# One overlapping read for the normalised tiles, and q, k, v weights in two row blocks of 256

## The chip, the cores and the metric

The kernel runs on one core of a Trainium2 chip. The metric is the time of one execution in microseconds of device time (us); lower is better. A core has engines with instruction queues of their own: PE (TensorE, matrix multiplication), DVE (VectorE), ACT (ScalarE), POOL (GpSimd) and SP (SyncE, which here only issues DMA transfers). They run at the same time and wait for each other through semaphores. A DMA transfer is issued by a queue (SP's or ACT's) and is then carried out by 16 DMA engines; who needs its data waits until the last share has landed.

## The reference

Two blocks share one normalised input, and both results are added to the input. S is 2048 tokens, D is 448 columns, 16 heads of 28 columns, a window of 256 tokens, F is 1792.

```python
def _A_ref(x, wqkv, wo):
    B, S, D = x.shape
    H = 16; Dh = D // H; W = 256
    qkv = (x @ wqkv).reshape(B, S, 3, H, Dh).transpose(2, 0, 3, 1, 4)
    q, k, v = qkv[0], qkv[1], qkv[2]
    scores = jnp.einsum("bhqd,bhkd->bhqk", q, k) * (Dh ** -0.5)
    idx = jnp.arange(S)
    mask = (idx[:, None] - idx[None, :] >= 0) & (idx[:, None] - idx[None, :] < W)
    p = softmax(jnp.where(mask[None, None], scores, -1e9))
    o = jnp.einsum("bhqk,bhkd->bhqd", p, v)
    return o.transpose(0, 2, 1, 3).reshape(B, S, D) @ wo

def _B_ref(x, w_gate, w_up, w_down):
    return (gelu(x @ w_gate) * (x @ w_up)) @ w_down

xn = _layernorm(x)
return x + _A_ref(xn, A_wqkv, A_wo) + _B_ref(xn, B_w_gate, B_w_up, B_w_down)
```

All tensors are bfloat16; sums are kept in float32.

## The kernel before, in words

**Tiling.** The tokens are 16 tiles of 128 rows (`x_sb`), handled in four blocks of 512 tokens (`qb` 0 to 3). A tile is normalised (`norm`, L169) into `xn`, turned by 90 degrees into `xnT` (128 partitions x 4 chunks x 2048 tokens), and `xnT` then feeds every matmul that contracts over the 448 columns of x. 448 is seven pieces of 64, while a partition dimension holds two pieces. So three chunks of `xnT` hold pieces 0 to 5 in pairs, and chunk 3 holds piece 6 in both halves. Of a contraction over 448, three matmuls take 128 rows each and one takes the last 64. Two such last halves, of different outputs, stand in the two halves of the array at once: one uses the upper copy of piece 6, the other the lower copy. For the feed-forward matmuls and for the projections of blocks 1 to 3, all seven pieces run as 64-row matmuls, two outputs beside each other; there each half of the array needs all seven pieces, its own ones from `xnT` and the other half's from `xsw`, a copy of `xnT` with the halves exchanged, which DMA makes (`swap`, L479). `wvs` and `wsq` are the weights for these exchanged pieces.

**How piece 6 comes into both halves.** For tiles 4 to 15, `norm` writes 512 columns with two DVE instructions (L174): 448 columns, and then the last 64 once more. The tile is turned by a DMA transpose (`dma_transp`, L186). For tiles 0 to 3 only 448 columns are written; PE turns them (`transp`, L190), the fourth transpose reading columns 320 to 447, and then POOL copies piece 6 from the upper to the lower half for all four tiles (L779, 64 x 512).

**Weights.** `wv` holds the v weights, `wraw` the q and k weights as loaded, both with four chunks. `wqp`, `wkp` and `w3p` hold q and k again, with each head padded from 28 to 32 columns: `pads` (L747) copies three chunks for groups of four heads, L790 copies the last 64 rows into `w3p`. The four spare columns of each padded head carry the last heads; `fill_pads` (L292) writes these, out of `wraw` and out of the small tile `w3k`.

**The first loads.** SP issues, in this order: tile 0 of x, tiles 2 and 3 (ACT issues tile 1), `wv` rows 0 to 383, the q and k columns of the first four heads (rows 0 to 383), tiles 4 to 7 of x in one transfer (L92), then the rows 384 to 447 of q, k and v (L94, L96; four transfers of 64 rows, v's twice), the other columns of q and k (L98), `wu`, and the two halves of `w3k`. Eight semaphores tell of landings in turn, so that a transfer is issued only when the one eight places ahead has landed (DMAHW0 to DMAHW7 in the lists below).

**Order of work.** Everything runs on one written order (a manual schedule). It begins with ten matmuls on zeros (`warmup`), statistics and normalisation of tiles 0 to 3 on DVE, their transposes on PE, v for tiles 0 to 3 (`v_dense` for three chunks, `v_half` for the fourth), q and k of the first four heads (`proj`, `qk_halves`), and then attention of block 0. In between DVE computes the statistics of tiles 4 and 5 (`stat`, L153, written before `qk_halves`). From there PE alternates between scores (L686), the product with v (L660) and pieces of other matmuls that a plan deals out. Tiles 4 to 7 are normalised during attention of block 0, tiles 8 to 11 in its feed-forward part, tiles 12 to 15 in that of block 1.

## Time and profile before

| | |
|---|---|
| median of 3 runs | 211.53 us (211.53 to 211.76) |
| the profiled execution | 211.63 us, of which its span is 209.9 us |
| PE busy | 204.2 us (97% of the span) |
| DVE busy | 156.4 us (75%) |
| ACT busy | 134.9 us (64%) |
| POOL busy | 42.0 us (20%) |
| DMA | 15.68 MB in 24890 packets, 9208 of them under 512 B |

The span runs from the first to the last instruction of the profiled execution; 1.73 us of its time lie around it. The granted PE clock stands at 9 tenths or more in all 40 slices. The DMA engines are nearly full from 2 us to about 20 us, and lightly loaded after 60 us. A row of the list in order of time gives the start, the time from the first start to the last end, the engine, the line, the operation, what it writes and reads, the shape and how many instructions are merged; behind it stands, in brackets, how long the engine had been idle and what ended that. PE's matmuls are pipelined, so their durations overlap.

### The profile page before, as it was taken

To read this page: it belongs to the slowest core of one execution; us is meant where nothing else is said; L and a number is where in the kernel's file an instruction comes from. 1 tells how busy PE (TensorE), PEld (TensorE's weight loads), DVE (VectorE), ACT (ScalarE), POOL (GpSimd) and SP (SyncE) were. 2 spreads that over 40 slices of the span, in tenths; PEclk is the share of its full clock that TensorE was granted. 3 is DMA by queue.
4 is the path that set the end of the run, shared out by engine and by line. 5 is a ranking of instruction groups with operands and counts; after the bars stand their busy time and mean duration, and the time that the engine had idled before them with its cause. 6 is when DMAs were issued, how large, how long until landed. Compare 5 with 4: busy or idle time off the path is not lost. (4 is left out here: it accounts for less than half of the span.)

```text
span 209.9 us, 6659 instructions
## 1 busy us (share of the span) xinstructions
PE 204.2 (97%) x2837; PEld 98.0 (47%) x2842; DVE 156.4 (75%) x359; ACT 134.9 (64%) x133; POOL 42.0 (20%) x77
## 2 busy tenths in 40 slices
PE   7899999999999999999999999999999999999994
PEld 2343444544454545444445444544444454544572
DVE  6898899899788984797438897395385699596532
ACT  4799896866677977423777788522587787756000
POOL 5368902241000220040000102012000022041000
PEclk9999999999999999999999999999999999999999
DMA  6999789983341001003331000100000010100011
GB/s 170 277 233 217 148 179 222 283 263 72 84 107 40 25 22 22 8 5 70 71 76 47 25 3 25 22 3 22 22 3 0 5 47 3 48 5 16 3 47 50
DMA packets 24890, 15.68 MB, mean 75 GB/s; under 512 B 9208, under 2 KB 24728, under 8 KB 24856
## 3 DMA queue, kind: packets, MB, share of 16 engines
q1 hardware_dynamic: 24712, 15.10, 31.2%
q8 instruction: 23, 0.38, 0.8%
q10 hardware_dynamic: 144, 0.11, 0.2%
q14 instruction: 11, 0.09, 0.2%
HBM read 9.26 MB, written 2.41 MB: 56 GB/s over the span
## 5 line engine op out<-in xcount | busy, mean ns | idle before, releaser
L691 ACT ACTIVATE p_sb<-sc 128x2048 bf16<-128x2048 f32 x38 | 71.4, 1879 | 16.9 <-PE sc L686 11.7
L543 ACT ACTIVATE p_sb<-gt 128x1024 bf16<-128x1024 f32 x28 | 28.6, 1026 | 31.3 <-PE gt L503 26.9
L503 PE MATMUL gt<-xnT,wg 64*128 64x512 bf16 x224 | 45.6, 376 | 0.0
L626 POOL TENSOR_TENSOR oN<-oc,l 128x512 bf16<-128x512 f32 x16 | 20.7, 1298 | 121.6 <-DVE l L639 121.6
L412 PE MATMUL po<-wd,hT 128*128 128x448 bf16 (+1 forms) x224 | 44.7, 347 | 0.0
L503 PE MATMUL gt<-xsw,wg 64*128 64x512 bf16 x168 | 40.7, 376 | 0.0
L611 DVE TENSOR_TENSOR p_sb<-p_sb,masks 128x256 bf16<-128x256 bf16 (+1 forms) x98 | 30.9, 369 | 7.4 <-ACT p_sb L691 7.4
L553 DVE TENSOR_TENSOR hT<-p_sb,u 128x512 bf16<-128x512 bf16 x34 | 21.7, 675 | 13.3 <-PE u L503 13.3
L412 PEld LDWEIGHTS <-hT 128*128 128x128 bf16 x238 | 21.9, 98 | 19.1 <-issue 2.2
L503 PEld LDWEIGHTS <-wg 64*128 64x128 bf16 x392 | 19.0, 94 | 22.3
L503 PEld LDWEIGHTS <-wu 64*128 64x128 bf16 x392 | 18.7, 94 | 22.2 <-issue 0.4
L503 PE MATMUL u<-xnT,wu 64*128 64x512 bf16 x136 | 28.1, 376 | 0.0
L503 PE MATMUL u<-xsw,wu 64*128 64x512 bf16 x102 | 24.7, 376 | 0.0
L503 PE MATMUL ue<-xnT,wu 64*128 64x512 bf16 x88 | 18.0, 377 | 0.0
L645 DVE TENSOR_TENSOR oc<-oc,ov 128x512 f32<-128x512 f32 (+1 forms) x16 | 10.4, 656 | 10.0 <-ACT oc L643 9.9
L503 PE MATMUL ue<-xsw,wu 64*128 64x512 bf16 x66 | 16.3, 377 | 0.0
L686 PE MATMUL sc<-qT,kT 28*64 28x320 bf16 (+4 forms) x736 | 16.2, 259 | 0.0
L400 DVE TENSOR_TENSOR res<-po,x_sb 128x448 bf16<-128x448 f32 (+1 forms) x14 | 8.1, 605 | 7.8 <-PE po L412 6.7
L686 PEld LDWEIGHTS <-kT 28*64 28x64 bf16 x736 | 8.1, 103 | 12.2 <-issue 11.0
L520 DVE CAST hT<-ue 128x512 bf16<-128x512 f32 x16 | 10.5, 685 | 2.8 <-PE ue L503 2.8
L643 ACT COPY oc<-ov 128x512 f32<-128x512 f32 x16 | 9.3, 585 | 4.0 <-PE ov L660 4.0
L639 DVE STREAM_TRANSPOSE l<-inv_all 128x512 f32<-128x512 f32 x16 | 11.1, 702 | 0.1
(115 smaller groups left out, 253.2 us busy)
## 6 DMA issues: line engine op xcount, KB each, us to landing
out_dram<-res SPq DMA_DIRECT2D x15, 112.0 KB
wd<-in_B_w_down_dram SPq DMA_DIRECT2D x2, 784.0 KB
x_sb<-in_A_x_dram SPq DMA_DIRECT2D x3, 448.0 KB
xsw<-xnT SPq DMA_DIRECT2D x6, 192.0 KB
wg<-in_B_w_gate_dram SPq DMA_DIRECT2D x2, 560.0 KB
wu<-in_B_w_up_dram SPq DMA_DIRECT2D x4, 224.0 KB
wu<-in_B_w_up_dram SPq DMA_DIRECT2D x2, 336.0 KB
wraw<-in_A_wqkv_dram SPq DMA_DIRECT2D x2, 252.0 KB
```

The lines of the kernel that those rows point to most:

```text
L412: nc.tensor.matmul(po[:, 0:w], lhsT=x[:, k, tt * P:(tt + 1) * P], rhs=wt[:, k, lo:up], start=start and n == 0, stop=stop and n == len(term ...
L503: nc.tensor.matmul(ps, lhsT=w[64 * hi:64 * hi + 64, c, p * P:(p + 1) * P], rhs=xchunk(qb, hi, c, qb * QB, QB), start=c == 0, stop=c == 6, ...
L520: copy(out=hTs[qb][:, p + 7 * i, :], in_=us[i])
L543: nc.scalar.activation(out=ges[p][:, :, :], in_=gt[:, :, :], func=ACT.Gelu_apprx_tanh)
L553: nc.vector.tensor_tensor(out=hT[:, p + 7 * i, :], in0=ge[:, i, :], in1=u, op=ALU.mult)
L611: nc.vector.tensor_tensor(out=reg, in0=reg, in1=m, op=ALU.mult)
L626: nc.gpsimd.tensor_tensor(out=oN[:, g, :], in0=oc[:, :], in1=inv, op=ALU.mult)
L639: nc.vector.transpose(out=l1[:, :, :], in_=inv_all[:, 4 * qb + g, :].unsqueeze(2).to_broadcast([P, 16, 32]))
L643: nc.scalar.copy(out=oc[:, :], in_=ov[0][:, :])
L645: nc.vector.tensor_tensor(out=oc[:, q0:], in0=oc[:, q0:], in1=ov[1][:, q0:], op=ALU.add)
L686: nc.tensor.matmul(ss[k0:k0 + nk, j, col:col + nq], lhsT=kT[r, g, kt * P + k0:kt * P + k0 + nk], rhs=qT[r, g, ring(qb).start + q0:ring(qb) ...
L691: nc.scalar.activation(out=p_sb[:, :, 0:ncol], in_=ss[:, :, 0:ncol], func=ACT.Exp, scale=SCALE)
```

## The change

The seven pieces of 64 columns are laid out anew. A tile of 512 columns now holds columns 192 to 447 and then columns 0 to 255, so that piece 3 (columns 192 to 255) stands twice: in the lower half of chunk 0 and in the upper half of chunk 3. (Before, piece 6 stood in both halves of chunk 3.)

For tiles 4 to 15 `norm` is one DVE instruction whose input pattern reads the tile in two rows of 256 columns, the second starting 192 columns before the first. For tiles 0 to 3 it still writes 448 columns, and the four PE transposes start at columns 192, 320, 0 and 128; POOL's copy at L779 is gone. Contractions that use the one half take chunks 0 to 2 whole and the low half of chunk 3; the others take chunks 1 to 3 whole and the high half of chunk 0. So q and even v tiles use the first form, k and odd v tiles the second.

The weights follow: one helper, `qkv`, loads rows 192 to 447 into chunks 0 and 1 and rows 0 to 255 into chunks 2 and 3, for v, and for the first and the other columns of q and k. The 64-row transfers and `w3k` are gone. Each of q, k and v thus has 512 rows loaded instead of 448. `w3p` is filled by `pads3`, one instruction for each half: the first four heads by ACT (two copies of 64 x 112), the other twelve by POOL (two of 64 x 336), where one ACT copy of 128 x 448 stood. `wvs` is copied from `wv` on the chip, and no longer loaded from memory. Which pieces are a half's own changes in the tables `OWN` and `SWAPPED`; the number of matmuls of each form stays the same.

```diff
+OWN = ({3: 0, 5: 1, 0: 2, 2: 3}, {4: 0, 6: 1, 1: 2, 3: 3})
+SWAPPED = ({4: 0, 6: 1, 1: 2}, {5: 0, 0: 1, 2: 2})
...
+    def qkv(dst, c0, c1):
+
+        for i in range(2):
+            nc.sync.dma_start(out=dst[:, 2 * i:2 * i + 2, :], in_=A_wqkv[192 - 192 * i:448 - 192 * i, c0:c1].rearrange("(c p) n -> p c n", p=P))
+
+    def columns(lo, up, k):
+
+        qkv(wraw[:, :, k * D + lo:k * D + up], k * D + lo, k * D + up)
+
...
-    nc.sync.dma_start(out=wv[:, 0:3, :], in_=rows(A_wqkv, 0, 3)[:, :, 2 * D:3 * D])
-    for c in (0, D):
-        nc.sync.dma_start(out=wraw[:, 0:3, c:c + 4 * Dh], in_=wqk[:, :, c:c + 4 * Dh])
+    qkv(wv, 2 * D, 3 * D)
+    columns(0, 4 * Dh, 0)
+    columns(0, 4 * Dh, 1)
     nc.sync.dma_start(out=x_sb[:, 4:8, :], in_=xv[:, 4:8, :])
-    for a in range(2):
-        nc.sync.dma_start(out=wraw[64 * a:64 * a + 64, 3, 0:D], in_=A_wqkv[384:448, a * D:(a + 1) * D])
-    for a in range(2):
-        nc.sync.dma_start(out=wv[64 * a:64 * a + 64, 3, :], in_=A_wqkv[384:448, 2 * D:3 * D])
-    for c in (0, D):
-        nc.sync.dma_start(out=wraw[:, 0:3, c + 4 * Dh:c + D], in_=wqk[:, :, c + 4 * Dh:c + D])
+    for k in range(2):
+        columns(4 * Dh, D, k)
...
-    w3k = const.tile([P, 4 * Dh], bf16, name="w3k")
-    for a in range(2):
-        nc.sync.dma_start(out=w3k[64 * a:64 * a + 64, :], in_=A_wqkv[384:448, D + 12 * Dh:2 * D])
...
-        xf = xn[:, :, :].rearrange("p a b -> p (a b)")
-        both = ((0, D, 0), (D, 64, 384))
-        for lo, n, src in both if t > 3 else both[:1]:
-            nc.vector.tensor_scalar(out=xf[:, lo:lo + n], in0=x_sb[:, t, src:src + n], scalar1=mv_all[:, t, 0:1],
-                                    scalar2=rstd_all[:, t:t + 1], op0=ALU.subtract, op1=ALU.mult)
+        x = x_sb[:, t, :]
+        to = xn[:, :, :].rearrange("p (i a) b -> p i (a b)", i=2)
+        if t > 3:
+            x = bass.AP(x.tensor, x.offset + 192, [list(x.ap[0]), [-192, 2], [1, 256]])
+        else:
+            x, to = x, xn[:, :, :].rearrange("p a b -> p (a b)")[:, 0:D]
+        nc.vector.tensor_scalar(out=to, in0=x, scalar1=mv_all[:, t, 0:1], scalar2=rstd_all[:, t:t + 1], op0=ALU.subtract, op1=ALU.mult)
...
-        for c, lo in enumerate((0, P, 2 * P, D - P)):
+        for c, lo in enumerate((192, 320, 0, P)):
...
     def v_dense(t, pv, first=True):
-        mm3(pv, lambda c: xnT[:, c, t * P:(t + 1) * P], lambda c: wv[:, c, :], first, not first)
+        m = t % 2
+        mm3(pv, lambda c: xnT[:, m + c, t * P:(t + 1) * P], lambda c: wv[:, m + c, :], first, not first)
...
+    def pads3(gs, eng=nc.gpsimd.tensor_copy):
+
+        for hi in range(2):
+            r, hs, c0 = slice(64 * hi, 64 * hi + 64), slice(4 * gs.start, 4 * gs.stop), D * hi
+            src = wraw[r, 3 - 3 * hi, c0 + Dh * hs.start:c0 + Dh * hs.stop]
+            eng(out=w3p[r, hs, 0:Dh], in_=src.rearrange("p (h d) -> p h d", d=Dh))
...
-    nc.gpsimd.tensor_copy(out=xnT[0:64, 3, 0:QB], in_=xnT[64:128, 3, 0:QB])
...
-    nc.scalar.copy(out=w3p[:, :, 0:Dh], in_=wraw[:, 3, 0:D].rearrange("p (h d) -> p h d", d=Dh))
+    pads3(slice(0, 1), nc.scalar.copy)
     nc.vector.memset(masks[:, 0, 0, 0:1], 1.0)
     make_masks(slice(0, 6))
+    pads3(slice(1, 4))
...
-        wv64 = A_wqkv[0:3 * P, 2 * D:3 * D].rearrange("(c h p) n -> h p c n", h=2, p=64)
         for hi in range(2):
-            nc.sync.dma_start(out=wvs[64 * hi:64 * hi + 64, :, :], in_=wv64[1 - hi])
+            nc.sync.dma_start(out=wvs[64 * hi:64 * hi + 64, :, :], in_=wv[64 - 64 * hi:P - 64 * hi, hi:hi + 3, :])
```

SP's queue at the start of the program, before the change. The words in brackets are what an instruction waits for; a transfer that waits for DMAHW0 to DMAHW7 waits for the landing of the one eight places ahead.

```order
1 L85 DMA x_sb<-in_A_x_dram 128x448
2 L88 DMA x_sb<-in_A_x_dram 128x2x448
3 L89 DMA wv<-in_A_wqkv_dram 128x3x448
4 L91 DMA wraw<-in_A_wqkv_dram 128x3x112 x2
5 L92 DMA x_sb<-in_A_x_dram 128x4x448
6 L94 DMA wraw<-in_A_wqkv_dram 64x448
7 L94 DMA wraw<-in_A_wqkv_dram 64x448 [waits DMAHW0_49]
8 L96 DMA wv<-in_A_wqkv_dram 64x448 [waits DMAHW1_49]
9 L96 DMA wv<-in_A_wqkv_dram 64x448 [waits DMAHW2_49]
10 L98 DMA wraw<-in_A_wqkv_dram 128x3x336 [waits DMAHW3_49]
11 L98 DMA wraw<-in_A_wqkv_dram 128x3x336 [waits DMAHW4_49]
```

The same place after the change:

```order
1 L95 DMA x_sb<-in_A_x_dram 128x448
2 L98 DMA x_sb<-in_A_x_dram 128x2x448
3 L89 DMA wv<-in_A_wqkv_dram 128x2x448 x2
4 L89 DMA wraw<-in_A_wqkv_dram 128x2x112 x3
5 L89 DMA wraw<-in_A_wqkv_dram 128x2x112 [waits DMAHW0_49]
6 L102 DMA x_sb<-in_A_x_dram 128x4x448 [waits DMAHW1_49]
7 L89 DMA wraw<-in_A_wqkv_dram 128x2x336 [waits DMAHW2_49]
8 L89 DMA wraw<-in_A_wqkv_dram 128x2x336 [waits DMAHW3_49]
9 L89 DMA wraw<-in_A_wqkv_dram 128x2x336 [waits DMAHW4_49]
10 L89 DMA wraw<-in_A_wqkv_dram 128x2x336 [waits DMAHW5_49]
```

Tiles 4 to 7 of x move from the sixth place on SP's queue to the ninth, behind 112 KiB more of v weights and 56 KiB more of q and k weights.

POOL's queue around the masks of block 0, before the change (`lnv` and `rstd_all` are the inverse deviation of tile 5):

```order
12 L779 COPY xnT<-xnT 64x512 [waits DVE_49,Activation_49,Pool_49]
13 L115 AFFINE_SELECT masks<-masks 64x64 [waits DVE_49]
14 L115 AFFINE_SELECT masks<-masks 64x4x64 x3
15 L115 AFFINE_SELECT masks<-masks 64x64
16 L115 AFFINE_SELECT masks<-masks 64x4x64
17 L161 TENSOR_SCALAR lnv<-mv_all 128x1 [waits DVE_49,Pool_49]
18 L162 TENSOR_TENSOR rstd_all<-lnv,minus_half 128x1 [waits Pool_49]
```

And after it:

```order
12 L121 AFFINE_SELECT masks<-masks 64x64 [waits DVE_49]
13 L121 AFFINE_SELECT masks<-masks 64x4x64 [waits Pool_49]
14 L121 AFFINE_SELECT masks<-masks 64x4x64 x2
15 L121 AFFINE_SELECT masks<-masks 64x64
16 L121 AFFINE_SELECT masks<-masks 64x4x64
17 L766 COPY w3p<-wraw 64x12x28 [waits DMAHW3_49]
18 L766 COPY w3p<-wraw 64x12x28 [waits DMAHW4_49]
19 L164 TENSOR_SCALAR lnv<-mv_all 128x1 [waits DVE_49,Activation_49,Pool_49]
20 L165 TENSOR_TENSOR rstd_all<-lnv,minus_half 128x1 [waits Pool_49]
```

A copy ahead of the masks is gone, and two copies stand between the masks and the deviation of tile 5; each of them waits for a landing of `wraw`.

43 lines of the change are left out of this document (23 added, 20 removed).

## The prediction

> **What bounds the kernel now.** I read the page's slices first: is one engine full all the way, and where not?
>
> ```profile
> PE   7899999999999999999999999999999999999994
> ```
>
> PE is below nine tenths only in the first two slices (10.5 us) and in the last. Since a pipelined PE is shown busy a little too long, I then asked for the waits of PE alone, longest first (us in total, times, longest):
>
> ```profile
> PE wps L150 <- DVE wo L124: 1.4, 1, 1.4
> PE tp L197 <- ACT xn L182: 0.8, 1, 0.8
> PE pk L202 <- issue: 0.2, 1, 0.2
> PE pq L202 <- issue: 0.2, 1, 0.2
> ```
>
> These are all its waits: two at the start (before the warm-up, and for tile 1), and 0.4 us afterwards. So whatever makes DVE, POOL, SP or the DMA engines cheaper later on has at most 0.4 us to win, and the end moves only with what PE waits for at the start. The third view is therefore the list in order of time from 6.4 us, all engines:
>
> ```profile
> 6.41 0.40 PE L197 MATMUL tp<-ident,xn 128*128 128x128 bf16 x4 [0.83 <-ACT xn L182]
> 6.75 0.74 PE L202 MATMUL pv<-wv,xnT 128*128 128x448 bf16 x3
> 7.54 0.27 DVE L752 COPY wqp<-wraw 128x336 bf16<-128x336 bf16 x1
> 8.14 0.42 DVE L198 COPY xnT<-tp 128x512 bf16<-128x512 bf16 x1 [0.33 <-PE tp L197]
> 8.23 0.47 ACT L752 COPY wkp<-wraw 128x336 bf16<-128x336 bf16 x1
> 8.49 0.63 DVE L155 BATCH_NORM_STATS2 st<-x_sb 128x6 f32<-128x448 bf16 x1
> 8.62 0.82 PE L202 MATMUL s<-xnT,wqp 128*128 128x512 bf16 x3
> 8.73 0.61 POOL L779 COPY xnT<-xnT 64x512 bf16<-64x512 bf16 x1 [3.17 <-ACT wkp L752]
> 8.90 0.56 ACT L790 COPY w3p<-wraw 128x448 bf16<-128x448 bf16 x1 [0.19 <-DMA wraw<-in_A_wqkv_dram]
> 9.15 0.18 DVE L156 BATCH_NORM_AGGREGATE mv_all<-st 128x2 f32<-128x6 f32 x1
> 9.25 0.59 DVE L155 BATCH_NORM_STATS2 st<-x_sb 128x6 f32<-128x448 bf16 x1
> 9.37 0.29 ACT L164 ACTIVATE lnv<-mv_all,eps_t 128x1 f32<-128x1 f32 x1
> 9.41 2.18 POOL L115 TENSOR_SCALAR_AFFINE_SELECT masks<-masks 64x64 bf16<-64x64 bf16 x6
> 9.70 0.20 ACT L165 ACTIVATE rstd_all<-lnv 128x1 f32<-128x1 f32 x1
> 9.88 0.18 DVE L156 BATCH_NORM_AGGREGATE mv_all<-st 128x2 f32<-128x6 f32 x1
> 10.02 0.39 PE L208 MATMUL s<-xnT,w3p 64*128 64x512 bf16 x2
> 10.48 0.69 DVE L256 CAST kT<-s 128x512 bf16<-128x512 f32 x1 [0.41 <-PE s L208]
> 11.27 0.44 DVE L752 COPY wkp<-wraw 128x336 bf16<-128x336 bf16 x1
> 11.39 0.42 PE L686 MATMUL sc<-qT,kT 28*64 28x320 bf16 x16
> ```
>
> From 6.41 us PE has work without a break. The reader is to see what nearly holds it up. The first scores at 11.39 need `kT`, which DVE casts from 10.48 to 11.17; ahead of that cast, in DVE's order, stand the statistics of tiles 4 and 5 (8.49 to 10.06), whose input is the transfer that the change puts behind more weights. Now DVE waits 0.41 us for PE before the cast; that is the cover.
>
> **The change, part by part.** *Tiles 4 to 7 of x land later.* Their statistics start at 8.49 without a wait, so I take 8.49 as the landing, its latest. If they start at t, DVE needs 1.39 to the second aggregate (8.49 to 9.88), 0.10 to its next instruction (9.15 to 9.25), 0.69 for the cast, and PE follows DVE by 0.06 (8.56 to 8.62): scores at t + 2.24. The branch over ACT (Ln at t + 0.88, Exp, then the cast of `qT`, under 0.7) comes to about t + 2.1 and is not the longer one. Scores at 11.39 hold while t is at most 9.15: the cover is 0.66 us.
>
> Ahead of this transfer stand 112 KiB more for `wv` and 56 KiB more for q and k, 172 kB. What the DMA engines moved, by stretch (the last two columns are their busy share and GB/s):
>
> ```profile
> 0.00:6.10 6.10, 4.14 (x14) 1.42 (x14) 3.97 (x16) 2.79 (x6) 3.24 (x9) 1.00 0.68 184
> 3.40:3.90 0.50, 0.50 (x2) 0.15 (x1) 0.47 (x3) 0.00 (x0) 0.26 (x1) 1.00 0.91 178
> 3.90:6.10 2.20, 1.68 (x9) 0.53 (x7) 2.13 (x6) 1.50 (x5) 0.27 (x1) 1.00 0.98 270
> 6.25:6.75 0.50, 0.34 (x4) 0.23 (x5) 0.44 (x2) 0.47 (x4) 0.00 (x0) 1.00 1.08 359
> 6.70:8.50 1.80, 1.80 (x16) 0.95 (x14) 1.34 (x5) 1.68 (x6) 0.00 (x0) 1.00 0.95 253
> ```
>
> 172 kB take 0.64 us at 270 GB/s and 0.68 at 253, the two stretches in which `wv`, the first q and k columns and these tiles themselves move. So t is 9.13 to 9.17, and the scores are delayed by 0 to 0.02 us. The ends are 359 GB/s (0.48 us, no delay) and 178 (0.97 us, a delay of 0.31). I take 0.05 us, near the two middle rows, since a late landing costs and an early one gives nothing. Being issued later costs nothing by itself: SP needs about 0.5 us a transfer,
>
> ```profile
> 2.24 1.02 SPq L91 DMA_DIRECT2D wraw<-in_A_wqkv_dram  x2
> 3.30 0.49 SPq L92 DMA_DIRECT2D x_sb<-in_A_x_dram  x1
> ```
>
> so three more put it at about 4.9 to 5.4 us; 1.15 MB are queued ahead of it by then, and the engines had moved 1.12 MB only by 6.1 us (184 GB/s over 6.1 us), so they do not run dry. The wait of the second first-columns transfer of k is for tile 0 of x, which DVE has been reading since 3.05.
>
> A row that bears on the price: the q and k columns come in pieces of 224 bytes.
>
> ```profile
> DMA packets 601, 0.21 MB, mean 275 GB/s; under 512 B 487, under 2 KB 601, under 8 KB 601
> DMA packets 225, 0.18 MB, mean 359 GB/s; under 512 B 28, under 2 KB 225, under 8 KB 225
> ```
>
> The first row is the stretch 4.50 to 5.25, mostly such pieces, the second 6.25 to 6.75, nearly none: a quarter less, not half. The Trainium skill ("DMA: Bandwidth & Descriptors", Specifications) says that a piece under 512 B does not reach line rate, because it is read, modified and written; this speaks against loading more of them. If each piece of 224 bytes cost as much as one of 512, an estimate from that page, the 256 additional pieces would count for 131 kB instead of 57, the landing would come 0.29 us later at 253 GB/s, and the sum below would be 211.8 instead of 211.6. The first row does not bear that out.
>
> *v weights in two blocks.* `v_dense(0)` at 6.75 reads both blocks, its third matmul, some 0.4 us later, the second one. x and `wv` are 0.92 MB after the change, of 1.12 MB moved by 6.1: no wait, though the slowest share may come near. `pads` of q at 7.54 and of k at 8.23 follow 0.2 and 0.4 us of data behind: no wait.
>
> *ACT's `w3p`.* One copy (0.56) becomes two of 112 columns; by 336 and 448 columns (0.47, 0.56) a copy of 112 is about 0.29, two 0.58. The wait of 0.19 for the 64-row transfer goes, so they end at 9.3 (9.46 before); PE wants the result at 10.02.
>
> *POOL.* The copy of 0.61 is gone and the masks start near 8.6 and end near 10.8. The two copies of `w3p` are at most 0.61 each (the row of 512 columns), and wait for the other q and k columns. These had landed by 11.27 (`wkp` there ran without a wait); 112 KiB more, 115 kB at 253 GB/s, is 0.45: by 11.72 at the latest. POOL is done by 12.4 or so, and PE wants it here, at 13.72:
>
> ```profile
> 12.97 0.81 PE L202 MATMUL pk<-xnT,wkp 128*128 128x512 bf16 x3
> 13.72 0.39 PE L208 MATMUL pq<-xnT,w3p 64*128 64x512 bf16 x1
> ```
>
> Behind the copies wait the deviation of tile 5, which the second of the four norms ahead of the transposes reads, and the masks on the first exponentials, which nobody on PE reads before the scores of the next steps are through. *DVE's `wkp`* of the second group, now at 11.27, waits by the same 0.45 and ends at 12.2; PE wants it at 12.97. Queued behind it are a v cast and the copies for groups 3 and 4 (the row of 12.16 below); they run 0.45 later, and PE comes to them only after 13.72.
>
> *The overlapping read.* The group rows (count, then busy and mean ns):
>
> ```profile
> L174 DVE TENSOR_SCALAR xn<-x_sb,mv_all,rstd_all 128x448 bf16<-128x448 bf16 x15 | 6.9, 460 | 0.1
> L174 DVE TENSOR_SCALAR xn<-x_sb,mv_all,rstd_all 128x64 bf16<-128x64 bf16 x12 | 5.1, 429 | 0.0
> 12.16 0.38 DVE L752 COPY wqp<-wraw 128x672 bf16<-128x672 bf16 x1
> ```
>
> Twelve instructions go (5.1 us of DVE). The remaining ones grow by 64 columns: 0.02 us each by the copies of 336 and 672 columns (0.27, 0.38), 0.43 at worst, if the pattern breaks the rate. DVE wins 0 to 0.4 us a tile, 0.3 likely. Four of the tiles come ahead of the DMA transposes of block 1, eight in the gated parts; PE waits for neither. What hides it: the last exchanged copy of block 1 is issued here, and read here,
>
> ```profile
> 25.66 1.25 SPq L484 DMA_DIRECT2D xsw<-xnT  x2
> 30.50 0.48 PEld L337 LDWEIGHTS <-xsw 64*128 64x128 bf16 x6
> ```
>
> 3.6 us after the issue has ended. *`wvs`* from the chip and three transfers fewer on SP lie under the same cover. *PE* has as many matmuls of each form as before.
>
> **Sum.** The profiled execution took 211.63 us, span 209.9, 0.10 above the median of 211.53. Delay 0.05, nothing won on the path: span about 209.95, 211.6 for the median.
>
> **The rivals.** *Slower: x lands too late.* The same transfer, with a landing after 9.57 us (8.49 + 0.66 + 0.42), from which point the delay passes 0.42 us. For it: 178 GB/s where `wv` begins to move, and 16 shares of which the slowest counts. Against it: the other four rows. At 129 GB/s, below any row, it lands at 9.82 and the time is 212.2. *Slower: the overlapping read is slow.* Each of the four norms ahead of the transposes would have to take some 1 us more than the pair it replaces to use up the cover of 3.6 us; beyond it the time is 211.6 plus the rest, about 212.1 at 4.1 us. Against it: no row of this form does so. *Faster: PE's remaining waits go.* Both rows of 0.2 us vanish since DVE and SP are less loaded: 211.1. Against it: "issue" says that they wait for nothing shown, and no part of the change touches them.
>
> **How the numbers follow.** What can be told from no change is about 0.2%, 0.42 us. Forecast, no measurable change, 211.6: 0.73. Late x: 0.17. Slow read: 0.04. Faster: 0.06. That gives faster 0.06, same 0.73, slower 0.21. The range must reach 211.84 (the end of the unknown price) and further into the late landing, to 212.2; downwards half of the faster rival, 211.2. The likeliest case alone is 211.4 to 211.9.
>
> **What would show it.** Right: the statistics of tile 4 start between 9.0 and 9.3 and now wait for `x_sb`; the first scores at 11.4 to 11.5; norms of 512 columns near 0.40 us where nothing disturbs them; POOL's `w3p` copies over before 13; no new PE wait. Wrong: a PE wait for `wv` at 6.75 or 7.1, scores after 11.8, a PE wait for `xsw` near 29, or a span that moves without any of these.

## The result, and the profile after

The changed kernel is slower. In the first comparison its median was 212.26 us (212.07 to 212.87, 8 runs) against 211.56 us for the kernel before, a ratio of 1.0036 (95% interval 1.0026 to 1.0046). In a later comparison it was 212.00 us (211.83 to 212.25, 9 runs) against 211.52, a ratio of 1.0022 (1.0012 to 1.0032). So it loses 0.5 to 0.7 us. (Two executions far off, 300.61 us of the kernel two_norms and 1167.99 us of before_pool3, are left out of the medians and ranges below.) The forecast was no measurable change, at 211.6 us. The profiled execution took 212.47 us, span 210.7, 0.8 above the span before.

PE is as full as it was (the same 40 digits). The waits of PE alone, longest first (us in total, times, longest), now have one row more, the third:

```profile
PE wps L153 <- DVE wo L130: 1.4, 1, 1.4
PE tp L202 <- ACT xn L187: 0.8, 1, 0.8
PE sc L692 <- DVE kT L263: 0.4, 1, 0.4
PE pq L207 <- issue: 0.2, 1, 0.2
PE pk L207 <- issue: 0.2, 1, 0.2
```

The list in order of time shows what is behind it: rows of ACT, DVE, POOL and PE at the place that the prediction spoke of (start, duration, engine; in brackets the idle time before and what ended it).

```profile
8.78 0.58 ACT L766 COPY w3p<-wraw 64x112 bf16<-64x112 bf16 x2
9.65 0.63 DVE L158 BATCH_NORM_STATS2 st<-x_sb 128x6 f32<-128x448 bf16 x1 [1.08 <-DMA x_sb<-in_A_x_dram]
11.05 0.46 POOL L766 COPY w3p<-wraw 64x336 bf16<-64x336 bf16 x1 [0.21 <-DMA wraw<-in_A_wqkv_dram]
11.85 0.42 PE L692 MATMUL sc<-qT,kT 28*64 28x320 bf16 x16 [0.39 <-DVE kT L263]
11.97 0.47 POOL L766 COPY w3p<-wraw 64x336 bf16<-64x336 bf16 x1 [0.47 <-DVE wqp L759]
12.81 0.28 DVE L759 COPY wkp<-wraw 128x336 bf16<-128x336 bf16 x1 [0.83 <-DMA wraw<-in_A_wqkv_dram]
13.43 0.81 PE L207 MATMUL pk<-xnT,wkp 128*128 128x512 bf16 x3
```

The statistics of tile 4 wait for x and start at 9.65 instead of 8.49, 1.16 us later, and the first scores at 11.85 instead of 11.39. That is the first loss, 0.46 us. The chain between them is the predicted one: 2.20 us from the start of the statistics to the scores, where 2.24 was forecast.

0.46 us do not make the 0.8 of the span. To find the rest I compared the start of each PE matmul with the start of the same matmul before: the difference is 0.00 us until the first scores, 0.46 from there to 33 us, 0.78 from 38 us to the end. So a second loss of 0.32 us lies between 33 and 38 us, in attention of block 0, where q and k of block 1 are projected beside it. PE's waits do not list it. These are POOL's, DVE's and PE's rows there, first of before, then of after:

```profile
30.85 0.70 DVE L639 STREAM_TRANSPOSE l<-inv_all 128x512 f32<-128x512 f32 x1
31.48 0.60 DVE L238 CAST v_sb<-pv 128x448 bf16<-128x448 f32 x1
31.73 1.27 POOL L626 TENSOR_TENSOR oN<-oc,l 128x512 bf16<-128x512 f32 x1 [5.29 <-DVE l L639]
32.75 0.73 DVE L611 TENSOR_TENSOR p_sb<-p_sb,masks 128x256 bf16<-128x256 bf16 x2
34.04 0.68 DVE L256 CAST kT<-pk 128x512 bf16<-128x512 f32 x1
34.74 0.38 PE L351 MATMUL pq<-xnT,wqp 64*128 64x512 bf16 x1
34.77 0.37 PE L351 MATMUL pk<-xnT,wkp 64*128 64x512 bf16 x1
```

```profile
31.31 0.70 DVE L645 STREAM_TRANSPOSE l<-inv_all 128x512 f32<-128x512 f32 x1
31.94 0.60 DVE L245 CAST v_sb<-pv 128x448 bf16<-128x448 f32 x1
32.55 1.26 POOL L632 TENSOR_TENSOR oN<-oc,l 128x512 bf16<-128x512 f32 x1 [5.65 <-DVE v_sb L245]
33.20 1.09 DVE L617 TENSOR_TENSOR p_sb<-p_sb,masks 128x256 bf16<-128x256 bf16 x2
34.82 0.68 DVE L263 CAST kT<-pk 128x512 bf16<-128x512 f32 x1
35.20 0.38 PE L357 MATMUL pq<-xnT,w3p 64*128 64x512 bf16 x1
35.55 0.37 PE L357 MATMUL pk<-xnT,wkp 64*128 64x512 bf16 x1
36.73 0.62 DVE L617 TENSOR_TENSOR p_sb<-p_sb,masks 128x256 bf16<-128x256 bf16 x2
```

The reader is to follow one link after the other. POOL's first scaling of an attention output (`oN`, called the scale below) needs DVE's transposition of `l`. It starts 0.18 us after that before (31.55 to 31.73) and 0.54 us after it now (32.01 to 32.55). The two mask products on DVE, which run into the scale, then take 1.09 instead of 0.73 us (a later pair, with nothing on POOL, 0.62). The casts of q and k behind them come 0.32 us later than the shift of 0.46 alone would put them. The cast of `kT` frees the bank of PSUM (the memory that PE writes its sums to) into which the third pair of projections writes k, and this k half starts 0.05 us after the end of the cast in both profiles (34.72 to 34.77, 35.50 to 35.55). So it now comes 0.35 us behind its q half, where 0.03 us lay between them before. PE's next product with v is at 38.66 us, at 37.88 before. Before, the bank was free just in time, so nothing showed that it was close.

Most of the rest came about as forecast. The overlapping read costs nothing (x12: count, then busy and mean ns): 5.8 us for twelve tiles, where a tile's pair had a mean of 460 and 429 ns.

```profile
L180 DVE TENSOR_SCALAR xn<-x_sb,mv_all,rstd_all 128x512 bf16<-128x512 bf16 x12 | 5.8, 494 | 0.0
```

DVE is busy for 153.5 us instead of 156.4, and PE, the bound, wins nothing from it.

### The profile page after: what moved, and what is told of

Its sections match the earlier page's. It is cut to its first block, busy times and chain, and to the rows that moved or that the text cites. A ratio compares the mean times of both kernels' runs of the same rounds, so it can differ in the third digit from the quotient of the medians.

```text
span 210.7 us, 6649 instructions
## 1 busy us (share of the span) xinstructions
PE 204.6 (97%) x2837; PEld 97.9 (46%) x2842; DVE 153.5 (73%) x347; ACT 135.1 (64%) x134; POOL 42.5 (20%) x78
## 5 line engine op out<-in xcount | busy, mean ns | idle before, releaser
L697 ACT ACTIVATE p_sb<-sc 128x2048 bf16<-128x2048 f32 x38 | 71.4, 1879 | 16.8 <-PE sc L692 11.6
L509 PE MATMUL gt<-xsw,wg 64*128 64x512 bf16 x168 | 43.8, 376 | 0.0
L509 PE MATMUL u<-xsw,wu 64*128 64x512 bf16 x102 | 27.1, 376 | 0.0
L509 PE MATMUL ue<-xsw,wu 64*128 64x512 bf16 x66 | 17.4, 377 | 0.0
L158 DVE BATCH_NORM_STATS2 st<-x_sb 128x6 f32<-128x448 bf16 x16 | 9.8, 614 | 2.1 <-DMA x_sb<-in_A_x_dram 2.1
```

The source lines that it names most:

```text
L158: nc.vector.bn_stats(out=st[:, :], in_=x_sb[:, t, :])
L509: nc.tensor.matmul(ps, lhsT=w[64 * hi:64 * hi + 64, c, p * P:(p + 1) * P], rhs=xchunk(qb, hi, c, qb * QB, QB), start=c == 0, stop=c == 6, ...
L697: nc.scalar.activation(out=p_sb[:, :, 0:ncol], in_=ss[:, :, 0:ncol], func=ACT.Exp, scale=SCALE)
```

## The experiments

For each kernel the table gives its time, its ratio to the kernel before on the same chip, and, from its one profile, the start of PE's matmuls minus the start of the same matmuls in the profile of before (median in each stretch, us). The first column only tells when an execution got going (in most profiles tile 0 of x landed 0.1 to 0.2 us earlier than in that of before); a loss is a step from one column to the next.

| kernel | median us (range, runs) | ratio, 95% | 8-10 | 20-22 | 28-30 | 44-46 | 190-200 |
|---|---|---|---|---|---|---|---|
| changed, first | 212.26 (212.07-212.87, 8) | 1.0036 (1.0026-1.0046) | 0.00 | 0.46 | 0.46 | 0.78 | 0.78 |
| after_again | 212.00 (211.83-212.25, 9) | 1.0022 (1.0012-1.0032) | -0.15 | 0.07 | 0.07 | 0.40 | 0.39 |
| split_before | 212.62 (212.02-213.12, 6) | 1.0046 (1.0030-1.0061) | -0.19 | -0.19 | -0.19 | 0.71 | 0.77 |
| wide_before | 211.77 (211.49-212.53, 11) | 1.0015 (1.0003-1.0026) | -0.16 | 0.61 | 0.61 | 0.61 | 0.61 |
| late_stat | 213.37 (213.29-213.43, 5) | 1.0084 (1.0071-1.0097) | -0.02 | 1.42 | 1.42 | 1.75 | 1.75 |
| late_stat2 | 212.59 (212.42-212.83, 5) | 1.0052 (1.0039-1.0065) | -0.16 | 0.74 | 0.74 | 0.74 | 0.74 |
| x_half | 211.93 (211.77-212.79, 10) | 1.0024 (1.0015-1.0034) | -0.15 | -0.15 | -0.15 | 0.17 | 0.16 |
| x_half_pool1 | 211.68 (211.38-212.09, 11) | 1.0003 (0.9994-1.0011) | -0.03 | -0.03 | -0.03 | -0.02 | 0.47 |
| after_pool1 | 211.71 (211.60-212.49, 12) | 1.0015 (1.0005-1.0024) | -0.10 | -0.10 | -0.10 | -0.06 | -0.07 |
| before_less1 | 211.89 (211.76-212.01, 11) | 1.0013 (1.0004-1.0022) | -0.17 | -0.17 | -0.17 | 0.15 | 0.15 |
| before_pool3 | 211.55 (211.44-211.83, 11) | 1.0000 (0.9991-1.0008) | -0.19 | -0.18 | -0.18 | -0.18 | -0.19 |
| before_pool15 | 211.53 (1) | - | -0.12 | -0.12 | -0.12 | -0.11 | -0.11 |
| x_half_masks | 211.89 (211.76-212.23, 11) | 1.0018 (1.0009-1.0026) | -0.13 | -0.13 | -0.13 | 0.17 | 0.16 |
| two_norms | 212.18 (211.85-214.06, 11) | 1.0039 (1.0022-1.0055) | -0.04 | -0.04 | -0.04 | 0.29 | 0.28 |
| other_data | 212.34 (211.84-212.44, 5) | 1.0035 (1.0022-1.0049) | -0.16 | -0.16 | -0.16 | 0.16 | 0.16 |
| other_data2 | 211.92 (211.83-212.15, 11) | 1.0013 (1.0003-1.0023) | -0.16 | -0.16 | -0.16 | 0.16 | 0.16 |
| both_out | 211.69 (211.50-212.18, 11) | 1.0003 (0.9991-1.0015) | -0.15 | 0.41 | 0.41 | 0.44 | 0.43 |

The theory was: x lands late through the bytes (or through the later issue) and costs the first loss; the scale's late start costs the second. The rivals were the overlapping read, other waits behind the late weights, and a landing that has nothing to do with it.

### Is x late through its place in the queue, or through the bytes?

*split_before*: the kernel before with as many issues ahead of x as the changed kernel has.

```diff
-    nc.sync.dma_start(out=wv[:, 0:3, :], in_=rows(A_wqkv, 0, 3)[:, :, 2 * D:3 * D])
-    for c in (0, D):
-        nc.sync.dma_start(out=wraw[:, 0:3, c:c + 4 * Dh], in_=wqk[:, :, c:c + 4 * Dh])
+    for r in (slice(0, 2), slice(2, 3)):
+        nc.sync.dma_start(out=wv[:, r, :], in_=rows(A_wqkv, 0, 3)[:, r, 2 * D:3 * D])
+    for c in (0, D):
+        for r in (slice(0, 2), slice(2, 3)):
+            nc.sync.dma_start(out=wraw[:, r, c:c + 4 * Dh], in_=wqk[:, r, c:c + 4 * Dh])
```

> The kernel before with its first v, q and k loads cut in two (chunks 0 and 1, then chunk 2): three issues more ahead of the transfer of x tiles 4 to 7, not one byte more, the pieces as they were. It is then issued at about 4.8 us instead of 3.30, as in the changed kernel. If the place in the issue queue makes x late (the engines run dry before its descriptors come), the statistics of tile 4 start at 9.3 to 9.6 us instead of 8.49, the first scores at 11.5 to 11.85 instead of 11.39, and the time is 0.15 to 0.5 us above before. If only the bytes ahead count, as the prediction had it, they start at 8.5 to 8.7 and the time is that of before within 0.1 us.

*wide_before*: the kernel before with the surplus bytes ahead of x, and no issue more.

```diff
-        nc.sync.dma_start(out=wraw[:, 0:3, c:c + 4 * Dh], in_=wqk[:, :, c:c + 4 * Dh])
+        nc.sync.dma_start(out=wraw[:, 0:3, c:c + 8 * Dh], in_=wqk[:, :, c:c + 8 * Dh])
...
-        nc.sync.dma_start(out=wraw[:, 0:3, c + 4 * Dh:c + D], in_=wqk[:, :, c + 4 * Dh:c + D])
+        nc.sync.dma_start(out=wraw[:, 0:3, c + 8 * Dh:c + D], in_=wqk[:, :, c + 8 * Dh:c + D])
```

> The kernel before with 224 instead of 112 columns of q and of k in the first loads: 172 kB more ahead of x tiles 4 to 7, which is the surplus of the changed kernel, by the same number of issues at the same times, in 448-byte pieces. If bytes alone set the landing, x lands 0.6 us later (172 kB at 275 GB/s), at 9.1 us, the statistics of tile 4 start there, the cover of 0.66 us just holds, and the time stays within 0.1 us of before. If bytes cost more than that, as a landing at 9.6 us in the changed kernel would have it if the issue had no part, the statistics start at 9.5 to 9.7 and the time is 0.4 to 0.5 us above before.

The statistics of tile 4 in split_before (the issue of x is above them), then PE's wait in its list, then the statistics in wide_before and PE's wait there:

```profile
4.72 0.43 SPq L94 DMA_DIRECT2D x_sb<-in_A_x_dram  x1
8.68 0.63 DVE L157 BATCH_NORM_STATS2 st<-x_sb 128x6 f32<-128x448 bf16 x1 [0.30 <-DMA x_sb<-in_A_x_dram]
31.39 0.74 PE L339 MATMUL pv<-wvs,xsw 64*128 64x448 bf16 x5 [0.54 <-DMA xsw<-xnT]
```

```profile
9.63 0.63 DVE L155 BATCH_NORM_STATS2 st<-x_sb 128x6 f32<-128x448 bf16 x1 [1.22 <-DMA x_sb<-in_A_x_dram]
10.63 0.39 PE L208 MATMUL s<-xnT,w3p 64*128 64x512 bf16 x2 [0.70 <-ACT w3p L790]
```

An issue 1.42 us later (3.30 to 4.72) let the statistics start 0.19 us later than in the profile of before, and 172 kB more ahead of x 1.14 us later, nearly as in the changed kernel (1.16). These starts lie where the second expectation (bytes that cost more) and the second half of the first (only the bytes count) put them; neither expected time came about. By these two rows alone it would be the bytes. But they are one profile each, and a row shows only the last of the 16 shares in which a transfer lands. The traces hold the time of every share (us; the middle is the mean of the 8th and the 9th; "as before" are before, before_less1, before_pool3 and before_pool15, "as changed" are all kernels with the changed kernel's first loads):

| first loads | profiles | middle share of x | 15th | last |
|---|---|---|---|---|
| as before | 4 | 7.14 to 7.45 | 7.64 to 8.38 | 7.90 to 8.47 |
| split_before: issued later | 1 | 8.06 | 8.43 | 8.66 |
| wide_before: more bytes | 1 | 7.59 | 8.07 | 9.61 |
| as changed: both | 9 | 8.28 to 8.48 | 8.56 to 9.30 | 8.85 to 9.68 |

The late row of wide_before is that of one share: fifteen had landed by 8.07 us, and the last share of `wv`, ahead of the additional bytes, was already 1.2 us behind its fifteenth (6.48 after 5.26). The middle share, which varies little, was 0.28 us later with the bytes alone, 0.75 with the later issue alone and 1.07 with both, each against the mean of the four old ones. So the greater part of the delay of x goes with the later issue, and the last share then adds something that changes from run to run. With one profile for each of the two kernels the parts are estimates. What the DMA engines moved until x had landed (the last two columns are their busy share and GB/s), before, in the changed kernel, wide_before and split_before:

```profile
2.00:8.46 6.46, 5.62 (x32) 2.31 (x29) 4.84 (x15) 4.46 (x13) 1.92 (x3) 1.00 0.98 271
```

```profile
2.00:9.62 7.62, 6.79 (x37) 2.85 (x35) 4.95 (x16) 5.26 (x15) 2.79 (x6) 1.00 0.95 271
6.00:7.00 1.00, 0.59 (x6) 0.39 (x7) 0.86 (x4) 0.94 (x5) 0.00 (x0) 1.00 0.64 132
```

```profile
2.00:9.61 7.61, 6.78 (x38) 2.82 (x35) 4.95 (x16) 4.70 (x13) 2.84 (x6) 1.00 1.00 282
```

```profile
2.00:8.65 6.65, 6.65 (x33) 2.82 (x31) 4.95 (x16) 4.70 (x13) 2.04 (x4) 1.00 0.85 239
```

The mean rate is the same before and after, 271 GB/s. Moved were 1.75 MB before (6.46 us by 271) and 2.07 MB after. The transfers up to x and x itself are 1.43 and 1.61 MB; so 0.32 MB of transfers issued behind x had gone through ahead of its last share before, and 0.46 MB after (wide_before 0.54, split_before 0.16). While one share is late, the others go on with what stands behind. From 6 to 7 us the engines ran dry for a while after the change (0.64 of their time, 132 GB/s), which the prediction denied. They did so with the later issue alone too (split_before 0.61 and 179 GB/s), and not with the early one (1.03 in before, 1.07 in wide_before).

split_before was slow all the same, through a wait that I had not listed: its last exchanged copy of block 1 is issued at 27.05 us instead of 25.66, and PE waits 0.54 us for it (the step in the table is 0.90). The prediction put the cover at 3.6 us from the end of the issue; but the copies land about 1.6 us after that (issue over at 27.88, last share at 29.48 in the changed kernel), and here one share was late again: fifteen had landed by 29.95 us, the last at 31.34. wide_before lost its 0.77 us in the profile with two waits at once, for x and, on ACT, for the last rows of q and k, that stand behind x; the row of PE above shows the second. Its 11 runs go from 211.49 us (no loss) to 212.53, so these landings change from run to run.

### The changed kernel without the wait for x

*late_stat*: the statistics move behind what PE wants.

```diff
-    stat(4)
-    rstd(4, 1)
-    stat(5)
-    rstd(5, 1)
     qk_halves(0, 0, pq, pk)
...
     pads(nc.vector.tensor_copy, wqp, slice(1, 2))
+    stat(4)
+    rstd(4, 1)
     v_copy(0, pvs[0], nc.scalar.copy)
     v_copy(1, pvs[1], nc.scalar.copy)
     pads(nc.vector.tensor_copy, wkp, slice(1, 2))
+    stat(5)
+    rstd(5, 1)
```

> The changed kernel with the statistics of tile 4 behind the first kT cast and the q pads of group 1, and those of tile 5 behind the k pads of group 1, so that nothing ahead of the first scores waits for x tiles 4 to 7. If that wait alone cost the first 0.46 us, the first scores start at 11.39 us. What then comes last is the k columns of heads 4 to 15, which landed at 12.71 us in the changed kernel: their pads end at 13.08, where TensorE without the first wait wants them at 12.76. So I expect a new wait of 0.3 to 0.4 us at the k projection of group 1 and a gain of only 0.05 to 0.15 us on the changed kernel. If the k columns don't come last, the gain is the whole 0.46. The second loss, 0.31 us in block 1, should stay if it hangs on something else than the start.

The first scores started at 11.37 as expected, but 1.44 us were lost behind them. ACT's list and PE's waits in this kernel:

```profile
12.24 0.29 ACT L167 ACTIVATE lnv<-mv_all,eps_t 128x1 f32<-128x1 f32 x1 [1.24 <-DVE mv_all L159]
12.68 0.95 ACT L245 CAST v_sb<-pv 128x448 bf16<-128x448 f32 x2
```

```profile
PE pq L207 <- ACT v_sb L245: 0.8, 1, 0.8
PE sc L692 <- ACT p_sb L697: 0.4, 1, 0.4
```

I had moved the wait on DVE and left its follower on ACT ahead of two v copies. ACT waits 1.24 us for the statistics, and PE for the PSUM banks of those copies, then for the exponentials (`p_sb`) behind them. The expectation was wrong for that reason. (The k columns were in time in this profile.)

*late_stat2*: so the scaling factors move too.

```diff
     pads(nc.vector.tensor_copy, wqp, slice(1, 2))
     stat(4)
...
-            plan = [[last_v, lambda: stat(6), (u, 3), ahead], [(u, 2), ahead2, (u, 2)], [(u, 1), ahead3, (u, 7)], [(u, 8), lambda: stat(8)],
+            plan = [[last_v, lambda: stat(5), lambda: rstd(4, 2), lambda: stat(6), (u, 3), ahead], [(u, 2), ahead2, (u, 2)], [(u, 1), ahead3, (u, 7)], [(u, 8), lambda: stat(8)],
```

> The changed kernel with the statistics of tile 4 behind the first kT cast and the q pads of group 1, those of tile 5 and the scaling factors of both (on ScalarE now, two GpSimd instructions less) behind the last v copy, so that neither VectorE nor ScalarE nor GpSimd waits for x tiles 4 to 7 ahead of work that TensorE wants. The late x then costs nothing where it did: the first scores start at 11.37 us. The k columns of the remaining heads, which landed between 11.67 and 12.71 us in the profiles of this layout, come next: a wait of 0 to 0.35 us at the k projection of group 1. With the second loss I expect 212.0 us, without it (the scale stands 66th) 211.7 us; 212.25 us if the late x was not the cause of the first loss.

Again the scores started in time, and again PE waited, later and for the same reason: ACT has to take q of group 1 and then the second exponentials behind the factors, which wait for DVE.

```profile
17.51 0.42 PE L692 MATMUL sc<-qT,kT 28*64 28x320 bf16 x16 [0.65 <-ACT p_sb L697]
```

0.90 us are lost there, none in block 1; the time, expected at 211.7 to 212.0 us, was 212.59. Both kernels show that the first wait is the late x, and neither gives its price, since each puts another wait in its place.

*x_half* keeps the order and makes x earlier.

```diff
-    nc.sync.dma_start(out=x_sb[:, 4:8, :], in_=xv[:, 4:8, :])
+    nc.sync.dma_start(out=x_sb[:, 4:6, :], in_=xv[:, 4:6, :])
     for k in range(2):
         columns(4 * Dh, D, k)
+    nc.sync.dma_start(out=x_sb[:, 6:8, :], in_=xv[:, 6:8, :])
```

> The changed kernel with x tiles 4 and 5 at the place where tiles 4 to 7 were loaded, and tiles 6 and 7 behind the remaining q and k columns: 229 kB instead of 459 kB to land before the statistics of tiles 4 and 5, and as many bytes less ahead of the columns. At the 320 GB/s that the changed kernel's transfers ran at from 7 us on, 229 kB are 0.7 us: tile 4 at about 8.9 us, the first scores at 11.39, the k columns at about 12.0 instead of 12.71, no wait at the k pads. Both theories of the late x then give 0.46 us below the changed kernel, 211.8 us; if the second loss in block 1 came from the first, 211.5, the time of before. If the time does not change, the late x is not the cause.

The statistics start at 8.33 us and the scores at 11.24, both without a wait; nothing is lost until 33 us. The second loss is still there in full, 0.32 us. The median is 0.33 us below that of the changed kernel in the first comparison and 0.07 below the second, so the wait for x is worth less in the median than the 0.46 us of the first profile.

### The place of the scale

In the profiles of the changed kernel, late_stat and x_half the scale was late, in those of before, split_before and wide_before in time, wherever DVE and the transfers stood. (late_stat2 has the new layout and an early scale; its POOL stream is three records shorter.) One thing in which the layouts differ is POOL's stream: one copy less, two copies more, two semaphore waits less. Counted in POOL's records, waits included, the scale is number 68 (from 0) after the change and number 69 before. *x_half_pool1* adds one instruction at the start, where POOL is idle; *before_pool3* adds three to the kernel before in the same way.

```diff
     nc.gpsimd.memset(v_sb[:, :, :, Dh + 1:32], 0.0)
+    spare_col = const.tile([P, 1], f32, name="spare_col")
+    nc.gpsimd.memset(spare_col[:, :], 0.0)
```

> The kernel x_half with one more tiny memset on GpSimd at the start, where that engine is idle, so that every later GpSimd instruction stands one place further back in its stream (the first scale as 69th counted from 0, as in the kernel before, and not as 68th). In three profiles of the new layout that scale started 0.50 us after its semaphores had passed, in three of the old layout 0.14 us. If the place in the stream makes the 0.36 us (instructions that come in groups of four, the first of a group late), it starts at 0.14 us again, the late PSUM bank behind it goes, and the time falls by about 0.3 us, to 211.6 us, the time of before. If the cause lies in what VectorE or the transfers do at that moment, nothing changes: 0.50 us and 211.9 us.

> The kernel before with three more tiny memsets on GpSimd at the start: the first scale stands three places further back (72nd counted from 0, again a multiple of four). If the place in the stream decides, it starts 0.50 us after its semaphores instead of 0.14, and the time rises by about 0.3 us, to 211.8 us. If it does not, the time is that of before, 211.5 us.

The scale and the mask products in x_half_pool1, then the scale in before_pool3:

```profile
31.70 1.27 POOL L635 TENSOR_TENSOR oN<-oc,l 128x512 bf16<-128x512 f32 x1 [5.29 <-DVE l L648]
32.72 0.74 DVE L620 TENSOR_TENSOR p_sb<-p_sb,masks 128x256 bf16<-128x256 bf16 x2
```

```profile
31.55 1.26 POOL L629 TENSOR_TENSOR oN<-oc,l 128x512 bf16<-128x512 f32 x1 [5.29 <-DVE l L642]
```

One idle memset brought the scale back to its time, the mask products to 0.74 us, and the median to 211.68 us, the time of before. (The profiled run of that kernel, 212.09 us, lost 0.50 us at 58 us, where PE waited for transfers into `oN`; nothing shows a link to either cause.) But number 72 is not late, so groups of four are out as the rule. Three more kernels: *after_pool1* is the changed kernel with the one memset alone. *before_less1* has one POOL instruction less ahead of the scale, number 68:

```diff
-        nc.gpsimd.memset(w3p[64:128, 12:16, :], 0.0)
+        nc.vector.memset(w3p[64:128, 12:16, :], 0.0)
```

*before_pool15* has fifteen more, behind that memset, number 84.

> The changed kernel with nothing but the one tiny GpSimd memset added. By the theory that the place of the first scale in GpSimd's stream makes the second loss, the scale starts 0.14 us after its semaphores, the loss of 0.32 us in block 1 goes and the late x stays: 212.26 - 0.3 = 211.95 us, with the first scores still at 11.4 to 11.85. If x_half_pool1 was faster for another reason, the time stays at 212.25 us.

> The kernel before with one GpSimd instruction less ahead of the first scale (the memset of w3p's pads behind the pad fills goes to VectorE): the scale stands 68th, as in the changed kernel. If that place alone makes it late, it starts at 0.50 instead of 0.14 us after its semaphores, and the time rises by about 0.3 us to 211.85 us. If it takes the changed kernel's own instructions as well, nothing moves: 211.55 us.

> The kernel before with fifteen tiny GpSimd memsets more, in the idle time ahead of the first scale, which then stands 84th. Place 72 was early, so a period of four is out. If the late places repeat every 8 or 16, the scale starts at 0.50 us after its semaphores here; if not, at 0.14 us. One look, for the place alone, not for the time.

The scale and the mask products in before_less1, and the q and k halves of the third pair; then the scale in after_pool1 (in before_pool15 it starts at 31.59 us):

```profile
31.92 1.27 POOL L626 TENSOR_TENSOR oN<-oc,l 128x512 bf16<-128x512 f32 x1 [5.66 <-DVE v_sb L238]
32.57 1.10 DVE L611 TENSOR_TENSOR p_sb<-p_sb,masks 128x256 bf16<-128x256 bf16 x2
34.57 0.38 PE L351 MATMUL pq<-xnT,wqp 64*128 64x512 bf16 x1
34.92 0.37 PE L351 MATMUL pk<-xnT,wkp 64*128 64x512 bf16 x1
```

```profile
31.63 1.26 POOL L634 TENSOR_TENSOR oN<-oc,l 128x512 bf16<-128x512 f32 x1 [5.29 <-DVE l L647]
```

before_less1 has nothing of the change and loses 0.32 us on PE and 0.33 us of median, at the same place, with the same two late rows and the same gap of 0.35 us. after_pool1 has the whole change and no second loss. So the second loss comes and goes with one POOL instruction ahead of the scale, in both layouts. In all nine profiles with a late scale it is number 68, in the nine others 65 (late_stat2), 69, 72 or 84; if it repeats, then not every 4, 8 or 16. The count takes in the waits: of the instructions that compute, 54 stand ahead of a late scale in before_less1 and of an early one in late_stat2.

Why number 68 is late stays open. The traces show one thing that goes with it. On the queue q14, which carries loads of instructions, a load of 8 KB starts between 23.2 and 27.4 us, ahead of the scale, in each of the nine profiles with an early one. In the nine with a late one it starts only behind the scale, between 36.0 and 38.7 us, and none stands between 22 and 35. So the instruction may act through where it puts such a load; the trace does not name the engine that the load is for, and no run tried it.

The rows tell how the late scale reaches PE. An early scale starts in the middle of DVE's v cast (31.73 within 31.48 to 32.08), a late one as the cast ends (32.55 after 32.54, 31.92 after 31.90); whether it waits for the cast, no run shows. DVE's mask products are the longer the more of the scale they overlap (undisturbed 0.62 us, 0.73 with 0.25 us of overlap, 1.09 with 0.61). In all 16 profiles with an overlap the two products end 0.48 us after the scale does. The Trainium skill ("SBUF — State Buffer", Who interferes with whom) says that VectorE and GpSimd share a pair of ports, that a VectorE instruction with two inputs from SBUF contends for it with a GpSimd instruction that reads SBUF, and that the one that issues first holds it to its end while the other waits. The mask products agree with that: their end follows the end of the scale, not their own start.

*x_half_masks* leaves the scale late and takes the mask products out of its way, by a second "masks" in the plan behind the casts of the first pair.

```diff
-                    [(w, 4), lambda: stat(11), lambda: rstd(8, 4), (w, 7), "masks", "sums", (w, 7), "inverse"]]
+                    [(w, 4), "masks", lambda: stat(11), lambda: rstd(8, 4), (w, 7), "masks", "sums", (w, 7), "inverse"]]
```

> The kernel x_half with the two mask products that collide with the first scale put behind the q and k casts of the first pair of block 1. If the second loss runs from the scale through the mask product to the casts and to the PSUM bank, as the traces suggest, the casts come at 32.6 us instead of 33.6 and the third pair of block 1 starts without a gap, even though the scale is as late as before: 211.6 us, 0.3 below x_half. If the casts are late for another reason, the time stays at 211.9 us.

The casts came at 33.30 us (33.61 in x_half), the third pair started without a gap, and the time did not change: 0.30 us were lost between 37 and 43 us instead, in the next product with v (1.31 us from first to last, 1.06 in x_half_pool1).

```profile
37.75 1.31 PE L667 MATMUL ov<-p_sb,v_sb 64*32 64x320 bf16 x72
37.81 0.63 DVE L264 CAST kT<-pk 128x512 bf16<-128x512 f32 x1
```

DVE is behind by what the masks now take later; its last `kT` cast, at 37.38 us in x_half_pool1, comes at 37.81. I take it that PE waits for the bank that this cast frees, as before; no run tried that.

### The overlapping read

*two_norms* undoes it in the changed kernel.

```diff
-            x = bass.AP(x.tensor, x.offset + 192, [list(x.ap[0]), [-192, 2], [1, 256]])
...
+        for to, x in ((xf[:, 0:256], x[:, 192:448]), (xf[:, 256:512], x[:, 0:256])) if t > 3 else ((xf[:, 0:D], x),):
+            nc.vector.tensor_scalar(out=to, in0=x, scalar1=mv_all[:, t, 0:1], scalar2=rstd_all[:, t:t + 1], op0=ALU.subtract, op1=ALU.mult)
```

> The changed kernel with the overlapping read undone: two products of 256 columns for each of tiles 4 to 15 instead of one of 512. Each pair should take VectorE about 0.3 us longer than the one (0.73 us for a pair in the profile of before against 0.40), beside other work. If the overlapping read has no part in the loss, the time is that of the changed kernel, 212.3 us within 0.2; if the wider read were the slow part, it falls towards 211.6 us.

```profile
L177 DVE TENSOR_SCALAR xn<-x_sb,mv_all,rstd_all 128x256 bf16<-128x256 bf16 x24 | 9.6, 450 | 0.0
```

9.6 us for twelve tiles against 5.8: 0.32 us a tile for the second instruction, beside other work. 212.18 us is the time of the changed kernel. The read has no part in the loss. In this profile x landed early enough (statistics at 8.90), and the second loss is there in full.

### Is that all?

*after_again* is the changed kernel once more. *other_data* and *other_data2* are the same kernel: they take the wait for x away and move nothing (tiles 4 and 5 are then normalised with the statistics of tiles 2 and 3).

```diff
-        nc.vector.bn_stats(out=st[:, :], in_=x_sb[:, t, :])
+        nc.vector.bn_stats(out=st[:, :], in_=x_sb[:, t - 2 if t in (4, 5) else t, :])
```

*both_out* has that and the memset.

> The changed kernel itself once more, beside the next one on the same chip, since its runs spread from 212.07 to 212.87 us: 212.0 to 212.5 us in the median. In its profile the scale is again 0.50 us after its semaphores (0.32 us on TensorE). If the landing of x varies from run to run, the statistics of tile 4 start between 8.9 and 9.7 us, and the loss ahead of the first scores is between 0 and 0.5 us: it need not be the 0.46 us of the first profile.

> The changed kernel with the statistics of tiles 4 and 5 taken from tiles 2 and 3, which have long landed: the same instructions in the same order on every engine, the same transfers, only the wait for x tiles 4 to 7 ahead of the first scores is gone (so the output of tiles 4 and 5 isn't the reference's). By the theory that the late x is the whole first loss and the place of the first scale the whole second one, the first scores start at 11.2 to 11.4 us, the second loss stays, and the time is that of the kernel before plus 0.32 us in every run: 211.85 us, with a spread as narrow as that of before. If the changed kernel has a third loss, the time stays at 212.1 us or above.

> The changed kernel with both causes out: the statistics of tiles 4 and 5 taken from tiles 2 and 3 (so tiles 4 and 5 of the output aren't the reference's), and the one tiny GpSimd memset that moves the first scale to place 69. If the late x and the place of the scale are the whole loss, the time is that of before within 0.15 us, 211.5 to 211.65 us, with as narrow a spread. If there is a third loss in some runs, as five unprofiled runs of other_data at up to 212.44 suggest, some runs stand 0.3 to 0.6 us above.

> The kernel other_data once more, on the same chip as both_out. By the two causes alone 211.85 us with a narrow spread; if a third, varying loss sits in this layout, runs between 212.0 and 212.5 us as before, and where the profiled run is such a one, its trace shows the wait.

In the profile of after_again the statistics start at 9.26 us and PE waits 0.16 us, a first loss of 0.22 us. Over all profiles with the changed kernel's first loads, x let the statistics start at 8.90 (two_norms), 8.96 (after_pool1), 9.26 and 9.65 us. other_data gave 211.84 us in its profile, with the second loss and nothing else, but its other four runs were 0.2 to 0.6 us higher, against the expectation; the repetition, with 11 runs from 211.83 to 212.15, met it. both_out is at the time of before (ratio 0.9991 to 1.0015; its median of 211.69 us is 0.04 above the expected range), so the two causes make up the loss of the median. Its profiled run was one of the slower ones, 212.12 us, and shows a third wait (DVE, then PE):

```profile
12.93 0.28 DVE L761 COPY wkp<-wraw 128x336 bf16<-128x336 bf16 x1 [1.42 <-DMA wraw<-in_A_wqkv_dram]
13.26 0.82 PE L209 MATMUL pk<-xnT,wkp 128*128 128x512 bf16 x3 [0.27 <-DVE wkp L761]
```

The other k columns came so late that PE waited for the pads, 0.44 us in all (the table's step of 0.56 has 0.12 more from 18 us on). It is the same kind of loss as the late x, from the transfers that stand next in the queue, and it too changes from run to run: these pads started at 11.6 to 12.9 us. In the changed kernel's own profile they ended at 13.09, where PE without the first loss would have wanted them at 12.97; there the late x hid it. Whether other_data's four slower runs were such runs is likely, and not shown, since they were not profiled.

Of the loss of 0.48 us (212.00 against 211.52) 0.32 are then the place of the scale, in every profile with it as number 68, and the rest the late landings, which cost 0 to 0.5 us; in the first comparison the landings cost more, 0.38 of 0.70. No version beats the kernel before: the changed one with the memset and the halved transfer of x comes to its time, the one with the memset alone stays 0.15 us above it in the median (interval 1.0005 to 1.0024).

## Why the prediction was wrong, point by point

- **"172 kB take 0.64 us at 270 GB/s and 0.68 at 253 ... I take 0.05 us", and "Being issued later costs nothing by itself".** This is the first step that failed: the cost of the landing. The rate was right (271 GB/s); the term put at nothing, the later issue, was not. It cost the middle share of x 0.75 us in split_before, the bytes 0.28 in wide_before, both together 1.07 (against 0.64 to 0.68). The statistics started 0.41, 0.47, 0.77 and 1.16 us later in the four profiles in which they waited for x, not by one value: the last share of 16 sets them, and it came at 8.85 to 9.68 us over nine profiles, at 7.90 to 8.47 over four with the old loads. And since a late landing costs and an early one gives nothing, the expected delay is a mean over the late ones (0.46, 0.22, 0 and 0 us in these four profiles, 0.17), even where the middle of the spread lies at the end of the cover.
- **The cover and the chain.** t + 2.24 was right to 0.04 us, and so was "scores at 11.4 to 11.5" as a consequence of t up to 9.3; after_again, with t = 9.26, has its scores at 11.46. The late-x rival was the right one for this part, its chance of 0.17 was too low, and its argument "other four rows against" compared rates, where the later issue and the slowest share decided. The sign "scores after 11.8" came (11.85), and so did a span that moves without a PE wait in the list.
- **"They do not run dry."** They did, from 6 to 7 us (0.64 of their time), as in split_before (0.61): 1.15 MB queued ahead did not keep all 16 engines busy until the data of x came.
- **"No new PE wait" after the start.** This is the second step that failed: 0.32 us, nearly as much as the landings in the first comparison (0.38) and twice as much in the second (0.16). "The end moves only with what PE waits for at the start" held for gains alone. The part on POOL counted durations and who wants the result, and held the scale of block 0 to be untouched, since no part of the change touches it. The change moved its number in POOL's stream. In the profile of before, the row of the mask products (0.73 us for two, with POOL's scale across it) and the distance of 0.03 us between the q and k halves of a pair could have told that nothing was left to spare there; not that one instruction less would use it.
- **DVE's `wkp`, "ends at 12.2; PE wants it at 12.97".** Mis-sized in the same way: 0.45 us was taken for the landing, 0.3 to 1.7 us were measured (pads from 11.61 to 12.93 us instead of 11.27). It became a wait in one profile.
- **Right:** ACT's two `w3p` copies (0.58), POOL's (0.46 and 0.47, over at 12.44, before 13), the overlapping read, `wvs`, no wait for `wv`, PE's two "issue" waits untouched. (The lower end of the range, "half of the faster rival", is 211.3 to 211.4 by its own figures, not 211.2; nothing hangs on it.)
- **The Trainium skill's rule on pieces under 512 bytes** ("DMA: Bandwidth & Descriptors", Specifications) gave, as an estimate, a landing 0.29 us later than the bytes alone, and a sum of 211.8. In the first profile the landing was later by more than that, in two of the four it was earlier than by the bytes alone. wide_before, with as many pieces as before at twice the size, was as late as the latest, so the runs do not show that the size of the pieces did it.
